# Per-pair reads for the output chains of a fused attention and ReGLU kernel, sixteen semaphores for the oT copies, and another static order

## The chip, the cores and the metric

The kernel runs on one core of a Trainium2 chip. The core has five engines that each work through an instruction queue of their own, in order: PE (TensorE, matrix multiplication; the profile shows its weight loads apart, as PEld), ACT (ScalarE), DVE (VectorE), POOL (GpSimd) and SP (SyncE, which here only issues DMA transfers). Engines wait for one another and for transfers through semaphores. The metric is the time of one execution on the device in microseconds (us). For the kernel before, the median of three runs is 687.94 us (687.48 to 688.73). Times inside the profile are counted from the start of its span.

## The reference

The input x is 2048 rows of 512 bfloat16 values. It is normalised row by row (layer norm without weights), and two blocks read the result; the output is the sum of both and of x:

```python
xn = _layernorm(x, axis=-1)
return x + _A_ref(xn, A_wqkv, A_wo) + _B_ref(xn, B_W_gate, B_W_up, B_W_down)
```

Block A is attention with 32 heads of 16 channels: `qkv = xn @ wqkv`, scores `q k^T` times 16^-0.5, softmax over all 2048 keys without a mask, times v, and `@ wo`. Block B is a gated ReLU layer with 1792 hidden channels: `relu(xn @ W_gate) * (xn @ W_up)`, and `@ W_down`. For each of the 32 heads 2048 x 2048 exponentials are needed.

## The kernel before, in words

**Tiling.** The 2048 rows are four chunks (c4) of 512 query rows. Within a chunk the 32 heads are eight groups of four heads, named by gg (0 to 3) and ee (0, 1); within a group the keys are 16 tiles of 128. For a chunk, a group and a key tile the scores of four heads are a tile of 128 x 2048. Most of them are made in two halves: a *unit* is one such half, a score pair on PE (`score`, L1289) into 128 x 1024 of PSUM, and one exponential on ACT (L1365) from there into a ring of 16 buffers in SBUF. There are 718 units, numbered in the order in which ACT does them; "sc190" is the score of unit 190. For 83 further tiles (`quad`, L1312) the exponential is made on DVE and POOL by integer arithmetic on the bits of a bfloat16: DVE copies the scores with a bias (L1320), then DVE (L1339) or POOL (L1335) adds two shifts. Both kinds are then weights for the products with v (`pv_stream`, L1244).

**Half operations.** PE's array is used as an upper and a lower half of 64 rows, which work side by side. A half operation is four matmuls (64 x 32 weights, 512 columns) on one half, with four weight loads ahead of it. Nearly all of PE's work is cut in this way: scores, products with v, the projections of q (`proj_q`, L837) and k (`proj_k`, L863), the gated layer (`glu`, L992) and the output rows (`out_rows`, L1034). PE has 5573 such operations and 12 blank ones that fill pauses.

**Output rows.** `out_rows` makes 128 rows of the output (index i in a chunk of four) as one chain that adds up in one PSUM bank: 14 pairs of a hidden tile hT and a piece of W_down, then up to four pairs of oT (the normalised attention output of a group, in x_sb) and a piece Wo_p of wo. Each pair is two half operations. W_down comes in 14 loads of 128 KB, six into Wd and four each into Wk and Wv, once these are no longer needed; a single tile object, t_wd, stands for all 14, and t_wo for the four loads of Wo_p. In the last chunk two of the row tiles (i = 1, 3) also add x through an identity pair, and end in `stream_out` (L1173), which the change leaves.

**Attention output.** When a group is done, `normalise` (L1188) copies the sums out of PSUM, sends the row sums through DRAM (streams n1, n2), and broadcasts the reciprocals back into rb with a transfer of 256 KB (stream n3, L1219). POOL multiplies (L1227, L1232). For the second group of each gg four small transfers of 16 KB (stream pk, L1234) bring the rows into oT. The q projections go through such copies of 16 KB too (L859, qT<-qf).

**What sets the order.** All operations are made as a graph of 8236 operations plus 12 blanks. The order of each queue and the places of the buffers come from a string, PLAN (L122 to L218), which `run` (L324) decodes; no planner runs at build time. `emit` (L380) then puts a wait wherever an operation depends on one whose semaphore its engine has not yet seen at that value, directly or through another engine. A half operation with weights waits for the writers of its weights ahead of its weight loads. `wait` (L476) emits one wait for each semaphore:

```python
for s, v in best.values():
    eng.wait_ge(s, v)
```

Each DMA stream has one semaphore; a load without a stream's name has one of its own, as each of the 14 loads of W_down and the four of Wo_p. Before a transfer of a stream is issued, the operations that read the transfer before it in that stream must have come far enough: SP waits for them. SP issues all transfers in one order.

**The opening.** x comes in as eight loads of one row tile (m = 0 to 7), two of two and one of four. wqkv comes as small parts for the first heads (Wq at L668, Wk at L669, 128 KB each), Wv (L672, 512 KB) and the rest of Wk and Wq (L685, L686, 384 KB each). PE transposes the normalised tiles of x (L764, through the identity), makes k and q for the first heads (L926) and then the first scores.

## Time and profile before

| what | value |
|---|---|
| median of three runs | 687.94 us |
| time of the profiled execution | 686.07 us |
| its span, first to last instruction | 684.2 us |
| PE busy | 675.6 us (99%) |
| PEld busy | 345.9 us (51%) |
| ACT busy | 666.8 us (97%) |
| DVE busy | 598.5 us (87%) |
| POOL busy | 499.8 us (73%) |
| granted TensorE clock, mean | 0.999 |

How to read the rows that follow in the prediction. A row of a timeline starts with the start in us from the start of the span and the length in us; then come engine, line of the kernel, operation, output<-inputs, number of instructions in the row, and in brackets the idle time of the engine before it with what ended it ("issue": nothing that the profile shows). Rows that begin with a line give a group: the shortest, median and longest duration in ns and the first and last start. A row with a window (from:to) gives the length, then busy time of PE, PEld, DVE, ACT and POOL with the number of instructions, the granted clock, the share of the DMA engines and GB/s. A row of a transfer ends with KB each and the median us from issue to landing. Matmuls overlap, so a row's length is that of a run of several.

### The profile page before, as it was taken

The numbers are of one execution on the slowest core, as the hardware profiler recorded it, in microseconds if no ns is written. First come the engines' busy times: TensorE is split into PE (matmuls) and PEld (weight loads), VectorE is DVE, ScalarE is ACT, GpSimd is POOL, SyncE is SP. The second block draws the span as 40 slices with busy tenths as digits, with TensorE's granted clock in tenths as the row PEclk, the third lists the DMA queues.
The fourth block names the chain that finished last, engine by engine and source line by source line (L and its number), as shares of the span: only waits on it lengthen the run. The fifth ranks groups of instructions, "written<-read, shape, count | busy, mean of one in ns | idle before, by whom it ended". The sixth has DMA issues, their size and how long they took to land.

```text
span 684.2 us, 45020 instructions
## 1 busy us (share of the span) xinstructions
PE 675.6 (99%) x22262; PEld 345.9 (51%) x19654; DVE 598.5 (87%) x1012; ACT 666.8 (97%) x730; POOL 499.8 (73%) x507
## 2 busy tenths in 40 slices
PE   8999999999999999999999999999999999999998
PEld 4455454545555554554444455554554455555543
DVE  9958899999989787999999788889998887988875
ACT  6999999999999999999999999999999999999994
POOL 3323768678688778887587886888878868787792
PEclk9999999999999999999999999999999999999999
DMA  7430220113122021212101022120202012131011
GB/s 216 57 75 12 58 77 27 33 55 91 56 65 66 5 77 34 69 41 63 35 23 31 10 78 63 38 69 5 56 27 61 25 53 62 44 86 42 22 36 54
DMA packets 55940, 35.86 MB, mean 52 GB/s; under 512 B 19336, under 2 KB 51784, under 8 KB 55752
## 3 DMA queue, kind: packets, MB, share of 16 engines
q1 hardware_dynamic: 55464, 32.71, 17.4%
q8 instruction: 164, 2.69, 1.6%
q10 hardware_dynamic: 288, 0.26, 0.1%
q14 instruction: 24, 0.20, 0.1%
HBM read 26.35 MB, written 2.35 MB: 42 GB/s over the span
## 4 chain that ended last, share of the span: by engine, by line
PE 75%; ACT 18%; DVE 5%; issue 1%; DMA 0%; POOL 0%; ACTq 0%
PE ps L250 75%; ACT ring L1365 18%; DVE stats L726 1%; DVE qd L1320 1%; DVE xn_sb L739 1%; DVE v_aug L876 0%; DMA x_sb<-in_A_x_dram 0%; DVE qT L952 0%; DVE mv L727 0%; ACT xn_sb L1164 0%; DVE qd L1339 0%; DVE xnT L780 0%; POOL rstd L721 0%; DVE xnT L1075 0%; DVE kT L869 0%
## 5 line engine op out<-in xcount | busy, mean ns | idle before, releaser
L1365 ACT ACTIVATE ring<-ps 128x1024 bf16<-128x1024 f32 x718 | 660.4, 1141 | 2.9 <-PE ps L250 2.5
L1335 POOL TENSOR_TENSOR qd<-qd,ints 128x512 int32<-128x512 int32 x446 | 450.5, 1041 | 143.8 <-DVE qd L1339 73.2
L250 PE MATMUL ps<-qT,kT 64*32 64x512 bf16 x8192 | 448.7, 374 | 1.3 <-DVE qd L1320 0.4
L1320 DVE TENSOR_SCALAR qd<-ps 128x512 int16<-128x512 f32 x612 | 396.7, 685 | 51.9 <-PE ps L250 49.0
L250 PE MATMUL ps<-qd,v_aug 64*32 64x512 bf16 x3672 | 263.0, 375 | 1.1 <-issue 0.9
L250 PE MATMUL ps<-ring,v_aug 64*32 64x512 bf16 x2872 | 236.5, 374 | 0.1
L1300 PEld LDWEIGHTS <-kT 64*32 64x32 bf16 x7584 | 151.1, 92 | 126.6 <-issue 32.6
L1272 PEld LDWEIGHTS <-v_aug 64*32 64x32 bf16 x4544 | 108.7, 91 | 75.6 <-issue 20.4
L250 PE MATMUL ps<-xnT,wgs 64*32 64x512 bf16 x1792 | 137.6, 374 | 0.0
L250 PE MATMUL ps<-xnT,wus 64*32 64x512 bf16 x1792 | 136.4, 374 | 0.0
L250 PE MATMUL ps<-Wd,hT 64*32 64x512 bf16 x768 | 59.0, 375 | 0.0
L810 PEld LDWEIGHTS <-wgs 64*32 64x32 bf16 x1792 | 43.1, 91 | 31.5 <-issue 7.4
L810 PEld LDWEIGHTS <-wus 64*32 64x32 bf16 x1792 | 43.2, 91 | 29.8 <-issue 7.6
L1339 DVE TENSOR_SCALAR qd<-qd 128x2048 int16<-128x2048 int16 x83 | 56.1, 690 | 2.3 <-PE ps L250 2.2
L810 PEld LDWEIGHTS <-hT 64*32 64x32 bf16 x1792 | 40.2, 92 | 28.2 <-issue 4.2
L250 PE MATMUL ps<-Wv,hT 64*32 64x512 bf16 x512 | 45.7, 375 | 0.0
L250 PE MATMUL ps<-Wk,hT 64*32 64x512 bf16 x512 | 42.8, 375 | 0.4 <-DVE qd L1320 0.3
L1020 DVE SCALAR_TENSOR_TENSOR hT<-ps,up_sb 128x512 bf16<-128x512 f32 x56 | 38.4, 685 | 4.6 <-PE ps L250 4.2
L1016 DVE COPY up_sb<-ps 128x512 f32<-128x512 f32 x56 | 38.4, 685 | 3.1 <-PE ps L250 2.5
L250 PE MATMUL ps<-Wo_p,x_sb 64*32 64x512 bf16 x480 | 40.2, 374 | 0.6 <-issue 0.5
L250 PE MATMUL ps<-xnT,Wq 64*32 64x512 bf16 x480 | 36.2, 375 | 0.0
L250 PE MATMUL ps<-xnT,Wk 64*32 64x512 bf16 x480 | 35.0, 374 | 0.3 <-DVE xnT L780 0.3
(70 smaller groups left out, 263.8 us busy)
## 6 DMA issues: line engine op xcount, KB each, us to landing
rb<-rec_scr SPq DMA_DIRECT2D x31, 256.0 KB
wus<-in_B_W_up_dram SPq DMA_DIRECT2D x38, 128.0 KB, 2.8
wgs<-in_B_W_gate_dram SPq DMA_DIRECT2D x38, 128.0 KB, 3.3
xr_sb<-in_A_x_dram SPq DMA_DIRECT2D x16, 128.0 KB, 2.6
qT<-qf SPq DMA_DIRECT2D x120, 16.0 KB, 2.6
out_dram<-xn_sb SPq DMA_DIRECT2D x14, 128.0 KB, 2.0
x_sb<-in_A_x_dram SPq DMA_DIRECT2D x8, 128.0 KB, 2.8
x_sb<-oT SPq DMA_DIRECT2D x60, 16.0 KB, 2.5
```

The lines of the kernel that those rows point to most:

```text
L250: return e.add_instruction(mybir.InstMatmult(name=e.bass.get_next_instruction_name(), engine=mybir.EngineType.PE, ins=[e.lower_ap(x), e.lo ...
L726: G.op("DVE", 580, lambda e, m=m: e.bn_stats(stats[:, m, :], xs(m)), reads=[t_xm[m]], writes=[t_st], prio=pr, order=last_xn if m == 4 else ())
L739: G.op("DVE", 320, lambda e, m=m, t=t_n: e.tensor_scalar(xn_sb[:, t.slot, :], xs(m), mv[:, m, 0:1], rstd[:, m:m + 1], op0=ALU.subtract, op ...
L810: e.ldweights(w()[rows, 32 * j:32 * j + 32], tile_position=(rows.start, 32 * j))
L1016: G.op("DVE", 603, lambda e: e.tensor_copy(up_sb[:, tup.slot, :], bank_of(tu)), reads=[tu], writes=[tup], prio=-590)
L1020: G.op("DVE", 603, lambda e: e.scalar_tensor_tensor(out=hT[:, th.slot, :], in0=bank_of(tg), scalar=0.0, in1=up_sb[:, tup.slot, :], op0=ALU ...
L1272: e.ldweights(vs(j), tile_position=(64 * half, 32 * j))
L1300: e.ldweights(ks(m), tile_position=(64 * half, 32 * m))
L1320: G.op("DVE", 601, lambda e, j=j, tx=tx: e.tensor_scalar(qd[:, tq.slot, 512 * j:512 * j + 512], ps[:, BANK[tx.slot], :], IBIAS[3], 0.0, op ...
L1335: G.op("POOL", POOL_NS / POOL_PIECES + 60, lambda e, x=x, n=n, c=slice(i * m, i * m + m): e.tensor_tensor(x().bitcast(I32)[:, c], raw().bi ...
L1339: G.op("DVE", 600, lambda e, n=n, x=x: e.tensor_scalar(x(), raw(), float(SHIFTS[n + 1]), None, op0=ALU.add), reads=[ti, tq], writes=[t], p ...
L1365: exp_ops[u] = G.op("ACT", 904, lambda e, tr=tr, k0=k0: e.activation(ring[:, tr.slot, :, :], ps[:, 4 * k0:4 * k0 + 2, :], ACTF.Exp, scale= ...
```

## The change: what it does

Three edits in the code, and another PLAN.

1. `mm_chain` takes a list of reads for each pair, where it is given one, and not only one list for the whole chain.
2. `out_rows` gives such lists: a pair with W_down reads its own hT tile and t_wd; a pair with Wo_p reads its own oT and t_wo; the identity pair reads its x rows and the identity. Before, each half operation of the chain read all of them.
3. The copies into oT use 16 streams (four for the partitions, four for gg) and not eight.

```diff
+            each = isinstance(reads[0], list)
...
+                mine = reads[i] if each else reads
                 for half in ((0, 1) if mode == "half" else (None,)):
                     fn, load = chain_part(w, x, lambda: bank_of(tile, sub), half, flags)
-                    G.op("PE", 216, fn, reads=reads, joins=[tile],
+                    G.op("PE", 216, fn, reads=mine, joins=[tile],
...
-                         load=load, weights=reads if weights is None else weights)
+                         load=load, weights=mine if weights is None else weights)
...
-            pairs, reads = [], [t_wo]
+            pairs, reads = [], []
             if first:
-                reads += [t_h[(c4, ft)] for ft in range(FT)] + [t_wd]
                 for ft in range(FT):
                     pairs.append(...)
+                    reads.append([t_h[(c4, ft)], t_wd])
             for g in gs:
                 to = t_oT[(c4, g)]
-                reads.append(to)
+                reads.append([to, t_wo])
...
+                reads.append([txr, t_id])
...
-                mm_chain(t, pairs, reads + [txr, t_id], pr, slots=slots, flags=flags)
+                mm_chain(t, pairs, reads, pr, slots=slots, flags=flags)
...
-                    stream=("pk", j, (n // 2) % 2), name="pk")
+                    stream=("pk", j, (n // 2) % 4), name="pk")
```

The new PLAN holds the same operations and as many blanks. Decoded and laid beside the old one:

- Of ACT's 731 operations all keep their place; of PE's 5573, 2286; of DVE's 1012, 791; of POOL's 503, 153; of SP's 429, 42. The shifts on average are 1.7 places on PE, 0.4 on DVE, 1.5 on POOL and 5.1 on SP; the largest are 106, 12, 28 and 47.
- 315 operations of PE stand in another unit. 143 of the 718 units hold another number of half operations. Units whose longer half holds five or more: 104 before, 98 after (20 of the 104 go, 14 others come).
- The first chain of chunk 0 starts in unit 226 (230 before), that of chunk 1 in unit 401 (402 before); the others start where they did. The first Wo_p pair of chunk 0 stands in unit 234 (237 before), that of chunk 1 in unit 404 (402 before).
- SP around unit 180: the broadcast of 256 KB that stood between two of the q copies for unit 190 stands behind them.
- The q copy with the least room stands in unit 489 for a score of unit 495 (471 before).
- The opening on SP, before: x0, x1, x2, x3, Wq, Wk, x4, x5, x6, x7, Wv, x8-9, x10-11, x12-15, rest of Wk, rest of Wq. After: x0, x1, x2, x5, x3, x4, x6, Wk, x7, Wq, x8-9, x10-11, x12-15, rest of Wq, rest of Wk, Wv.
- The opening on PE, before: the last four transposes stand in a row between the scores of units 2 and 3. After: the scores of units 1 to 5 stand between and behind them (only the last two transposes stay together). Seven blanks stand ahead of the first transpose, three before. The first half operation that reads Wv has place 51, 47 before.

More of the change, by code (lines that the diff above doesn't have):

```diff
@@ new lines @@
+    "cRBe3`v7izZ7n25-1k{zSRg-OUHhNre!~NXo5O5hiYegVn$H~HIP)hOqg%u1${eBl))61N9L9A>f5H0NyfB~EL0^g`b#rNBUhBeUna?i&g>5s&GjauEF>X4`jDuw{be|!9lZ<bn%jtCPA0<9@%Q)j("
+    "->$hFXFjQLYYyW9E;gncUvu-mdDAcsHs8Yx6gS;yOlVw42iX=jrxDYc7rJ@VKcQE(1x<`HT?YAtF^}IOX^>?(x1u8caAWJzFS=qTmtx-bU76l6Y&Lyh%xT2lG*;X)O_i5MJm9y3{_?2erfy`7&wG~d"
+    "ZQ0L#Nvr!EXPD>Po8fD28fgYfE+v<@PtI)tFiY5<qTJkwF^%+qFR@aYFW_P`TxYiM$VH9ZV9F;&X%q+<Y^1e6mHGdcoiDC(cFVcks#kf}3$xr5FJ$H^mI=(9#LN8;`fA-Q53@F`>@(uejJb>udLagR"
+    "<xaec!W1vFO>gd-zG7a58N2YBi+Rm_7kB7!?i<L(G~$B!QphX?Gbnz*vROtqQXBy=!wplJ*W5EVlZW{s%xmSD_(`lMzm!XxgN*Q5!0u%}m(X7+&SZy38u^rN6pC~M^P3=Y$S{MP#LR`{1%1ewePQOl"
@@ new lines @@
+    "yn~fEzQVRAxNl++0kJ*9$wmSsJHUnYUOApwA>igFt*v<(*{dWwlbt$X7I6Tu_{qh*_8Ot(!gzBInOf2#+}s;CZkx_!()qfs8V^W|%=GY@uxl=20Ff+B7{1lDWHs3-7(!$cStTFzS^y*FHgZ7PB!(!)"
+    "*0{_<qbv+Rn|2#%FEi1|KrZ8HIL7Z6ZVa-92Jnr)^a7ZMTVrGuG8<y}S;j0Z=An;dmjc5V<~pXGrpKhU<X0;OhUKyvxYydRfs84d;WwKv$Vc3_Q*KK|BR1SjPcLl7`%=gtIVH)ZBylIqx;2YhhMSxC"
+    "ZK)HZwu}(LH<3XPMi#;c8ZsB<y1EfB%VW9`b7qpP0<oOrT$3M6)RNC~U9r$gV6L&AC?v1QWv2Mc$QL;tpwVo}ZewlZLONNHjiLlVzfBGC0EHB&g8YyipsW0%klO?nhY!pGfHyF4xL=i+Ldrk0Vil~^"
+    "c7`(*y8!(}+R0HcW9)m@FB~m7<d=IkLgw6}an7v@*G*Wq%SL0gIo9uA8<qIYH$tUzpX%a%WolLp?4C1z)cu5Sr+2O>wr$uJF$PJD_Iu5e#CD2RY*X0S&o<65K?nDXTkhYQZ#(8KQ=#!d^Av8^^E^<?"
```

182 lines of the change are left out of this document (87 added, 95 removed).

## The prediction

> **What bounds the kernel now.** I read the page first (engines, chain, groups), then ACT's timeline around each stop, and there the timelines of PE's weight loads and of SP. The page:
>
> ```profile
> span 684.2 us, 45020 instructions
> PE 675.6 (99%) x22262; PEld 345.9 (51%) x19654; DVE 598.5 (87%) x1012; ACT 666.8 (97%) x730; POOL 499.8 (73%) x507
> PE 75%; ACT 18%; DVE 5%; issue 1%; DMA 0%; POOL 0%; ACTq 0%
> L1365 ACT ACTIVATE ring<-ps 128x1024 bf16<-128x1024 f32 x718 | 660.4, 1141 | 2.9 <-PE ps L250 2.5
> ```
>
> PE is named in three quarters of the chain and ACT is busy 97% of the span: both are nearly full, so the chain's shares don't say what a change is worth. The 718 exponentials of L1365 do. Their spacing, from ACT's timeline in a stretch without stops, and their first and last start:
>
> ```profile
> L1365 ACT ACTIVATE ring<-ps x718: 1017/1146/1314, 10.9 to 673.1; 128x1024 bf16<-128x1024 f32 x180
> 516.07 14.85 ACT L1365 ACTIVATE ring<-ps 128x1024 bf16<-128x1024 f32 x16
> 528.73 3.11 ACT L1365 ACTIVATE ring<-ps 128x1024 bf16<-128x1024 f32 x3
> ```
>
> The last two rows come from two windows: the second begins with the first one's fifteenth exponential, so (528.73-516.07)/14 = 0.904 us apart. 717 intervals at 0.904 make 648.2; the stream takes 673.1-10.9 = 662.2. So ACT loses 14.0 us to stops; 10.9 us lie before it and 684.2-673.1 = 11.1 behind its last start. A change pays here only if it removes stops of the exponentials or shortens those two ends. Times below are lost ACT time: the distance of two starts less 0.904 for each.
>
> **The change part by part.**
>
> *A. The waits at the start of an output chain.* Before, every half operation of out_rows reads one list (all 14 hT tiles, all of Wd, all of Wo_p, all oT copies). Thus the first half op of a chunk's chain waits for every semaphore of the list that PE has not yet seen. The rows of ACT and of the weight loads at the four chunk starts:
>
> ```profile
> 222.85 2.08 ACT L1365 ACTIVATE ring<-ps 128x1024 bf16<-128x1024 f32 x2
> 225.36 1.02 ACT L1365 ACTIVATE ring<-ps 128x1024 bf16<-128x1024 f32 x1 [0.42 <-PE ps L250]
> 381.54 1.21 ACT L1365 ACTIVATE ring<-ps 128x1024 bf16<-128x1024 f32 x1
> 383.77 1.94 ACT L1365 ACTIVATE ring<-ps 128x1024 bf16<-128x1024 f32 x2
> 540.73 3.02 ACT L1365 ACTIVATE ring<-ps 128x1024 bf16<-128x1024 f32 x3
> 542.54 2.13 ACT L1365 ACTIVATE ring<-ps 128x1024 bf16<-128x1024 f32 x2
> 631.49 3.01 ACT L1365 ACTIVATE ring<-ps 128x1024 bf16<-128x1024 f32 x3
> 632.51 1.07 ACT L1365 ACTIVATE ring<-ps 128x1024 bf16<-128x1024 f32 x1
> 224.21 0.12 PEld L810 LDWEIGHTS <-hT 64*32 64x32 bf16 x4 [0.73 <-DVE qd L1320]
> 382.40 0.12 PEld L810 LDWEIGHTS <-hT 64*32 64x32 bf16 x4 [0.68 <-DVE qd L1320]
> 541.80 0.12 PEld L810 LDWEIGHTS <-hT 64*32 64x32 bf16 x4 [0.43 <-DVE qd L1320]
> 631.36 0.34 PEld L810 LDWEIGHTS <-hT 64*32 64x32 bf16 x9 [0.36 <-DVE qd L1320]
> ```
>
> Chunk 0: 225.36-222.85 is two intervals and 0.70 more. Chunk 1: 383.77-381.54 is 0.42 too long for two. Chunk 2: 542.54-540.73 loses nothing. Chunk 3: 632.51-631.49 loses 0.12. The sum is 1.24. The DVE step that the rows name (qd, a score copy) has nothing to do with hT; the weight load was last in a row of waits. By the code chunk 0 has 16 DMA semaphores there: eight for Wd (six of its own, and one each for the part in Wk and the part in Wv, whose loads wait for one another), four for Wo_p, four for the oT copies. Chunks 1 to 3 have the eight semaphores of the copies and one or two of engines. The idle time goes with that number: 0.73 for sixteen, 0.36 to 0.68 for eight and a few.
>
> After the change a Wd half op waits for its own hT and for Wd. t_wd is still one tile of 14 loads, so chunk 0's first half op, now at unit 226 instead of 230, keeps eight DMA semaphores. Its first Wo_p half op, at unit 234, gets the four of Wo_p and four copies: eight again. The next three pairs have four copies each, since the copies now use 16 streams and not eight. (On SP that costs nothing: a copy there waits for a reader of the copy before it in its stream, which is now the one of the same heads a chunk earlier, read long before.) In chunks 1 to 3 the chain starts on hT alone, and each Wo_p pair waits for four copies. Queued behind such a wait on PE are the score half ops of the next units, and so ACT. Two groups of eight at the price of chunk 3 cost 2 x 0.12; groups of four I take at 0.05 in all (their nearest row, chunk 2, lost nothing). A = -1.24 + 0.24 + 0.05 = -0.95. Bounds: -1.24 if all of it hides as in chunk 2; 0 if the two groups and the groups of chunk 1 each cost the 0.42 of chunk 1 (1.26 against 1.24).
>
> *B. The q copies before unit 190.* SP's order, the landing times of such copies, and what ACT and PE did:
>
> ```profile
> 178.53 0.58 SPq L1219 DMA_DIRECT2D rb<-rec_scr  x1
> 179.15 1.16 SPq L859 DMA_DIRECT2D qT<-qf  x2
> DMA to landing us min/median/max: 1.7/2.6/5.6
> 184.97 0.41 PE L250 MATMUL ps<-qT,kT 64*32 64x512 bf16 x4 [0.40 <-DVE qd L1320]
> 184.65 1.09 ACT L1365 ACTIVATE ring<-ps 128x1024 bf16<-128x1024 f32 x1
> 186.10 1.02 ACT L1365 ACTIVATE ring<-ps 128x1024 bf16<-128x1024 f32 x1 [0.37 <-PE ps L250]
> ```
>
> The landing row is that of tile qT. The second copy was issued at about 179.7, behind a broadcast of 256 KB (rb), and the score that reads it ran at 184.97, some 5.2 us later, at the slow end of 1.7 to 5.6. ACT lost 186.10-184.65-0.904 = 0.55. The new order puts the broadcast behind these copies. It has its own reader on POOL (the multiplications of normalise), which has no exponential behind it directly. I take -0.45: 0.1 remains. Bounds: -0.55, and +0.55 if another copy gets the same stop, since nearly all of SP's instructions (387 of 429) change places.
>
> *C. The small stops.* Two rows of PE's timeline with score half ops give the length of a step:
>
> ```profile
> 12.01 0.38 PE L250 MATMUL ps<-qT,kT 64*32 64x512 bf16 x8
> 13.64 0.60 PE L250 MATMUL ps<-qT,kT 64*32 64x512 bf16 x16
> ```
>
> Eight matmuls are one step of both halves of the array, sixteen are two, and these take 0.22 longer. PE's two halves run side by side, so a unit (the work between two scores) takes as many steps as its longer half has. In 104 units of the old order that is five or more: at least 5 x 0.22 = 1.10 against ACT's 0.904. The new order has 98 (20 go, 14 come). Six fewer at 0.2 would give -1.2 if nothing covered them; but a shorter unit beside a long one covers some, so I take a third, -0.4. Bounds: -1.2, and +1.2 if those that come are uncovered and those that go were covered. POOL (350 of 503 instructions in other places) and DVE (221 of 1012) I cost at 0 within this term: POOL has slack (73% busy), and where that cover is gone the scores' copies on DVE are late next, at the same 0.2 a stop.
>
> *D. The opening.*
>
> ```profile
> 3.62 1.93 SPq L655 DMA_DIRECT2D x_sb<-in_A_x_dram  x4
> 8.49 1.03 SPq L686 DMA_DIRECT2D Wq<-in_A_wqkv_dram  x1
> Wq<-in_A_wqkv_dram SPq DMA_DIRECT2D x1, 384.0 KB, 7.6
> x_sb<-in_A_x_dram SPq DMA_DIRECT2D x2, 128.0 KB, 3.4
> 8.59 1.06 PE L926 MATMUL ps<-xnT,Wq 128*32 128x384 bf16 x32
> 10.91 2.87 ACT L1365 ACTIVATE ring<-ps 128x1024 bf16<-128x1024 f32 x3
> 12.33 1.36 PE L764 MATMUL ps<-ident,xn_sb 128*128 128x128 bf16 x16
> 14.10 3.82 ACT L1365 ACTIVATE ring<-ps 128x1024 bf16<-128x1024 f32 x4 [0.32 <-PE ps L250]
> 15.12 0.38 PE L250 MATMUL ps<-Wv,xnT 64*32 64x512 bf16 x4
> 15.00:16.20 1.20, 1.11 (x48) 0.67 (x48) 1.20 (x4) 1.20 (x3) 0.00 (x0) 1.00 0.09 29
> ```
>
> Gain: four transposes in one piece (12.33) hold the score of unit 3; 14.10-10.91 is three intervals and 0.48. The new order puts scores between them (only the last two stay together); I count -0.3, since DVE's and PE's work there is only spread. Loss: the small load of Wq moves from fifth to tenth in SP's queue. The x loads of the same size at that place (issued by 3.62+1.93) land after 3.4, so Wq at about 5.1+3.4 = 8.5 to 9.0, where the projection began at 8.59: 0 to 0.4, I take 0.2. Wv moves from the eleventh place to the last load. The last place now (Wq's rest, issued 8.49) lands 7.6 later at 16.1; the first Wv half op ran at 15.12 and has four places more before it, so about 15.5. PE then stands up to 0.6 us; the scores of units 4 and 5, which the new order puts ahead of that half op, give ACT two more exponentials (1.8 us), which covers half of it: +0.3. Behind 16.2 the queue is empty (the last row: DMA share 0.09). D = -0.3+0.2+0.3 = +0.2; bounds -0.5 (both loads in time) and +0.9 (no gain, 0.4 and 0.5 lost).
>
> [...]
>
> *E. Stops without a cause in the order.*
>
> ```profile
> 406.70 1.03 ACT L1365 ACTIVATE ring<-ps 128x1024 bf16<-128x1024 f32 x1
> 408.64 1.02 ACT L1365 ACTIVATE ring<-ps 128x1024 bf16<-128x1024 f32 x1 [0.92 <-PE ps L250]
> 407.51 0.09 PEld L1272 LDWEIGHTS <-v_aug 64*32 64x32 bf16 x1 [1.18 <-issue]
> ```
>
> The largest single stop (408.64-406.70-0.904 = 1.04) has "issue" as its cause: PE waited for nothing that the profile shows. The diff adds no instruction to PE except where waits move, so I cost this at 0, with ±1.0 because such a stop can fall elsewhere. The tail (stream_out, which the diff leaves) I cost at 0 too; its cover is that its half ops still read Wo_p and Wo_l as one list.
>
> Sum: A -0.95, B -0.45, C -0.4, D +0.2 = **-1.6 us**. The profiled run took 686.07, of which 684.2 is the span; it lies 1.87 below the median of 687.94, so I move the median: 687.94-1.6 = **686.3 us**. The bounds, added as they stand, are -4.5 and +3.7.
>
> **The rivals.**
>
> *Late copies (slower).* SP is one queue in order, and the new order shortens margins: the copy with the least (a q copy of unit 495) is issued 6 units ahead of its score (24 before), 6 x 0.904 = 5.4 us, against landings of up to 5.6 us in tile qT's row. If copies or weights come late like that of 184.97, each costs 0.55. Three such stops use up the 1.6; from six on the kernel is slower by the 0.2% (1.4 us) that a measurement here can tell from no change. Six give 687.94-1.6+3.3 = 689.6. For it: SP's order is new nearly throughout. Against it: only one stop of that kind stands in the trace of before, and the median landing is 2.6.
>
> *The waits only move (no difference).* The change then doesn't do what it says: chunk 0 keeps eight semaphores twice, and B's stop goes to another copy; then A is 0, B 0, C -0.4, D +0.2: 687.7. For it: the row of chunk 1, 0.42 with as few semaphores. Against it: chunks 2 and 3, with about as many, lose 0 and 0.12.
>
> *The order removes many small stops (faster by more).* Of the 14.0 us, the stops named above (1.24, 0.55, 0.48, 1.04) are 3.3; 10.7 remain in small pieces. If a quarter of these goes (2.7) in place of the 0.4 of C, the time is 687.94-1.6-2.3 = 684.0. For it: 143 of the 718 units get another number of half ops, so there is room for it. Against it: only 315 of 5573 PE instructions change their unit, and the number of units with five steps falls by six alone.
>
> **How the numbers follow.** Chances: the sum as it stands 0.44 (its own range 685.3 to 687.5), late copies 0.20, waits only move 0.16, many small stops 0.20. Faster by over 0.2%: all of the last and three fifths of the first, 0.47; slower: 0.20; the rest, 0.33, is within 0.2%. The range goes from 683.4 (a third of the small-stops case lies below) to 689.4 (somewhat over half of the late-copies case lies above), leaving out a little under 2 in 10.
>
> **What would show it.** A: no idle time of 0.6 before a weight load of hT in units 226 to 232 and 401 to 404; instead idle of 0.4 or less at the first hT load of chunk 0 and at its first x_sb load. B: no gap in the exponentials near 185. C: ACT's first-to-last start about 1.5 shorter than 662.2. D: an unbroken row of exponentials from the first to the sixth, or else a gap before the first Wv half op near 15.5. It is wrong if scores wait for q copies at new places, if ACT's first start moves beyond 11.4, or if stops of "issue" come to more than the one of 407.5 and its like.

## The result, and the profile after

The changed kernel takes 691.95 us in the median of six runs (690.60 to 693.70), against 687.50 for six runs of the kernel before beside it: a ratio of 1.0062 with a 95% interval of 1.0047 to 1.0077. It is slower by about 4.3 us, where 1.6 us less was forecast. The profiled execution took 691.17 us, 689.4 of it span, 5.2 more than before.

The page of the changed kernel (span, busy times, chain by engine, the group of the exponentials; L1368 is what L1365 was), and the row of the exponentials' line with shortest, median and longest duration and the first and last start:

```profile
span 689.4 us, 45023 instructions
PE 678.6 (98%) x22262; PEld 350.6 (51%) x19650; DVE 599.9 (87%) x1012; ACT 668.4 (97%) x730; POOL 499.8 (73%) x507
PE 91%; DVE 2%; POOL 2%; issue 1%; DMA 1%; ACT 1%; SPq 0%; ACTq 0%; POOLq 0%
L1368 ACT ACTIVATE ring<-ps 128x1024 bf16<-128x1024 f32 x718 | 662.2, 1138 | 4.9 <-PE ps L250 3.8
```

```profile
L1368 ACT ACTIVATE ring<-ps x718: 1018/1146/1316, 12.3 to 678.2; 128x1024 bf16<-128x1024 f32 x180
```

The busy times hardly move, and POOL, which had 0% of the chain, now has 2%. The first exponential starts 1.4 later and the last 5.1 later. To see where, I took the start of each exponential from the trace, subtracted 0.904 per interval, and added what is left over stretches of units. This table serves all the runs below; its columns are the first start, the four stretches, what lies behind the last start, and the span (one profiled execution each, us):

| kernel | first start | units 1-40 | 41-198 | 199-219 | 220-717 | tail | span |
|---|---|---|---|---|---|---|---|
| before | 10.91 | 1.14 | 3.36 | 0.32 | 9.18 | 11.11 | 684.2 |
| after | 12.27 | 1.96 | 2.27 | 1.60 | 11.93 | 11.17 | 689.4 |
| e1 changed code, old order | 11.84 | 1.11 | 3.00 | 0.32 | 10.98 | 11.04 | 686.5 |
| e2 new order, old opening | 11.79 | 1.07 | 2.97 | 2.05 | 12.02 | 11.17 | 689.2 |
| e3 new order, three blanks | 11.23 | 2.96 | 2.58 | 3.87 | 10.32 | 11.18 | 690.3 |
| e4 new order, 128 more | 13.33 | 1.91 | 3.38 | 2.10 | 8.32 | 11.21 | 688.4 |
| e5 new order, one copy earlier | 11.75 | 1.95 | 2.44 | 0.23 | 9.17 | 11.61 | 685.3 |
| e6 old opening, copy earlier | 11.51 | 1.19 | 2.85 | 0.11 | 10.58 | 11.17 | 685.6 |
| e7 as e6, 128 more | 11.09 | 1.13 | 3.91 | 0.18 | 7.67 | 12.07 | 684.2 |
| e8 before, 128 more | 11.13 | 0.98 | 2.97 | 0.40 | 11.43 | 11.03 | 686.1 |
| e9 old order, copy late | 11.51 | 1.13 | 2.58 | 3.57 | 10.96 | 11.04 | 689.0 |
| e10 as e6, 64 more | 11.68 | 2.03 | 2.76 | 0.38 | 9.25 | 11.17 | 685.4 |
| e11 as e6, 192 more | 11.68 | 1.10 | 3.27 | 0.23 | 8.73 | 11.18 | 684.3 |
| e12 as e6, more transfers | 11.03 | 1.38 | 5.63 | 0.10 | 14.89 | 11.16 | 692.4 |

After against before: the opening with the first 40 units +2.2, units 41 to 198 -1.1, units 199 to 219 +1.3, the rest +2.75. The gains lie at the places of A and B. The losses come from three causes: the opening, one oT copy with what follows from it, and the "issue" stops.

**The places of A and B** look as they should. ACT's rows at the q copies of unit 190 and at the two chain starts, then the first weight loads of hT and x_sb there (chunk 0, chunk 1):

```profile
179.00 13.98 ACT L1368 ACTIVATE ring<-ps 128x1024 bf16<-128x1024 f32 x15
221.49 11.25 ACT L1368 ACTIVATE ring<-ps 128x1024 bf16<-128x1024 f32 x12
378.74 13.99 ACT L1368 ACTIVATE ring<-ps 128x1024 bf16<-128x1024 f32 x15
222.59 0.12 PEld L810 LDWEIGHTS <-hT 64*32 64x32 bf16 x4 [0.31 <-issue]
229.39 0.12 PEld L810 LDWEIGHTS <-x_sb 64*32 64x32 bf16 x4
383.66 0.10 PEld L810 LDWEIGHTS <-hT 64*32 64x32 bf16 x4
386.73 0.12 PEld L810 LDWEIGHTS <-x_sb 64*32 64x32 bf16 x4 [0.25 <-issue]
```

The exponentials run on in all three stretches. The first hT load of chunk 0 stands 0.31 with its eight semaphores where it stood 0.73 with sixteen; chunk 1's hT starts without a wait, and its x_sb load stands 0.25. In PE's trace these waits are instructions of their own (EVENT_SEMAPHORE), two semaphores each and 0.106 us apart: six ahead of the load at 224.21 before, two ahead of the one at 222.59 after. The even steps show that none of them had to wait for anything; their number is the cost.

**The opening.** ACT, then PE (L910 and L1383 are the warm-up and the blanks), then SP's issue of Wv and its landing in the changed kernel; the last fence is the first transpose of the kernel before:

```profile
12.27 5.61 ACT L1368 ACTIVATE ring<-ps 128x1024 bf16<-128x1024 f32 x6
18.30 2.08 ACT L1368 ACTIVATE ring<-ps 128x1024 bf16<-128x1024 f32 x2 [0.42 <-PE ps L250]
5.43 2.54 PE L1383 MATMUL ps<-Wo_l 128*128 128x512 bf16 x7
7.81 0.61 PE L764 MATMUL ps<-ident,xn_sb 128*128 128x128 bf16 x8
17.00 0.38 PE L250 MATMUL ps<-Wv,xnT 64*32 64x512 bf16 x4
8.22 1.30 SPq L672 DMA_DIRECT2D Wv<-in_A_wqkv_dram  x1
Wv<-in_A_wqkv_dram SPq DMA_DIRECT2D x1, 512.0 KB, 7.6
```

```profile
5.52 0.40 PE L764 MATMUL ps<-ident,xn_sb 128*128 128x128 bf16 x4
```

The seven blanks hold PE until 7.81, so the first transpose comes 2.3 later than before; its input had been written at 5.65. Wv lands at 8.22 + 7.6 = 15.8, and ACT has a first stop of 0.61 at its seventh exponential. PE does not wait for Wv there: ahead of 17.00 stand two blanks and a pause for ACT.

**One oT copy.** Units 199 to 219 lost 1.28 more. SP, POOL and ACT of the changed kernel there, with PE's row between; L1239 is the copy into oT, L1222 the broadcast n3, L1219 the transfer n2, L1235 POOL's multiplication:

```profile
185.72 0.47 SPq L1219 DMA_DIRECT2D rec_scr<-rrec  x1
190.27 0.57 SPq L1222 DMA_DIRECT2D rb<-rec_scr  x1
190.88 0.57 SPq L1239 DMA_DIRECT2D x_sb<-oT  x1
195.81 1.28 POOL L1235 TENSOR_TENSOR oT<-o_sb,rb 128x512 bf16<-128x512 f32 x1 [2.44 <-DMA x_sb<-oT]
208.81 0.38 PE L250 MATMUL ps<-qd,v_aug 64*32 64x512 bf16 x4 [0.44 <-POOL qd L1338]
209.44 1.02 ACT L1368 ACTIVATE ring<-ps 128x1024 bf16<-128x1024 f32 x1 [0.24 <-PE ps L250]
```

And of the kernel before, the same copy (first of the two) and the same multiplication:

```profile
163.58 2.15 SPq L1236 DMA_DIRECT2D x_sb<-oT  x2
191.11 1.29 POOL L1232 TENSOR_TENSOR oT<-o_sb,rb 128x512 bf16<-128x512 f32 x1 [0.66 <-DVE qd L1339]
```

The copy, one of the four of chunk 0's first group, is issued at 190.88 where it was issued at 163.58: it stands behind n2 and n3, and n3 makes SP stand until n2 has landed (4.1 us here). The multiplication of unit 190's group writes the buffer that this copy reads, so POOL stands 2.44 for it. Behind it in POOL's order are the shifts of quad 200; PE waits for one of them with a product at 208.81, and the exponentials of units 212 and 213 come 0.35 and 0.30 late.

The larger part of the 1.60 came another way: unit 201 lost 0.76. DVE, PE and ACT of the changed kernel, and in the second fence the same shift on DVE before:

```profile
195.85 1.80 DVE L1342 TENSOR_SCALAR qd<-qd 128x2048 int16<-128x2048 int16 x1
198.30 0.59 PE L250 MATMUL ps<-qT,kT 64*32 64x512 bf16 x12 [0.57 <-DVE qd L1323]
198.98 10.23 ACT L1368 ACTIVATE ring<-ps 128x1024 bf16<-128x1024 f32 x11 [0.50 <-PE ps L250]
```

```profile
194.94 0.68 DVE L1339 TENSOR_SCALAR qd<-qd 128x2048 int16<-128x2048 int16 x1
```

By the code (`port` in `run`) POOL's shifts and multiplications wait for DVE's last shift, but a shift on DVE does not wait for POOL. Here DVE's shift starts 0.04 us behind the late multiplication, takes 1.80 us where the median of the 83 is 0.68, and ends 0.55 after the multiplication has. The score copy behind it is late, and so is a score. A second shift, at 207.94, takes 1.36 beside a shift on POOL. Such a shift of over 1.3 us stands in the traces of all five kernels with the late copy (after, e2, e3, e4, e9) and in none of the nine others, whose longest is under 1.0. So part of the copy's price is that POOL, once late, meets DVE.

**The "issue" stops.** The largest single loss of the changed kernel is 0.96 at unit 441. ACT's row, PE's row, and the page's row of the queue that fetches instructions (number of packets, MB, share):

```profile
422.13 3.77 ACT L1368 ACTIVATE ring<-ps 128x1024 bf16<-128x1024 f32 x4 [0.82 <-PE ps L250]
421.25 0.37 PE L250 MATMUL ps<-qd,v_aug 64*32 64x512 bf16 x1 [0.67 <-issue]
q8 instruction: 164, 2.69, 1.7%
```

PE broke off inside a row of four matmuls (three are there at 420.19) and waited for nothing the profile shows. PE and PEld have 22262 + 19650 = 41912 instructions on the page, and 41912/164 is about 256; 2.69 MB in 164 packets are 16 KB each. In the traces of before and after every packet of this queue has 16384 bytes, and from the start of one to the start of the next PE starts 256.0 and 255.6 instructions on average, its waits counted. So I read it as one fetch of 16 KB for each block of 256 of PE's instructions. Numbered in PE's order, nearly all such stops lie at numbers of about 190 to 202 within a block of 256, in every run. At them PE goes on 1.2 to 1.6 us after the end of a fetch, and at none of these borders in the two traces sooner (the least is 1.27 before, 1.20 after), as if a block could be used only then. By this reading stops at such borders cost the exponentials 2.2 us before and 6.5 after: 0.49 at unit 238, 0.45 at 242, 0.76 at 315, 0.96 at 441, 0.55 at 586, 0.52 at 603, and smaller ones. Two of these are not borders alone. At 238 and 586 PE stands at the waits for the copies of a Wo_p pair, and a border falls on them:

```profile
232.40 0.12 PEld L810 LDWEIGHTS <-x_sb 64*32 64x32 bf16 x4 [0.69 <-issue]
```

In the same order with the border elsewhere (e4) the two units lose 0.02 and 0.12. The sums below also depend on the counting: they take the stops from 0.05 us in the 2.7 us behind such a pause; taken from 0.14 us in 1.8 us they are 2.1 before and between 1.8 and 6.5 in the other traces without added traffic.

### The profile page after: what moved, and what is told of

It is laid out like the page before. It is cut to its first block, busy times and chain, and to the rows that moved or that the text cites. A ratio compares the mean times of both kernels' runs of the same rounds, so it can differ in the third digit from the quotient of the medians.

```text
span 689.4 us, 45023 instructions
## 1 busy us (share of the span) xinstructions
PE 678.6 (98%) x22262; PEld 350.6 (51%) x19650; DVE 599.9 (87%) x1012; ACT 668.4 (97%) x730; POOL 499.8 (73%) x507
## 3 DMA queue, kind: packets, MB, share of 16 engines
q8 instruction: 164, 2.69, 1.7%
## 4 chain that ended last, share of the span: by engine, by line
PE 91%; DVE 2%; POOL 2%; issue 1%; DMA 1%; ACT 1%; SPq 0%; ACTq 0%; POOLq 0%
PE ps L250 90%; POOL qd L1338 2%; DVE qd L1323 1%; DMA wgs<-in_B_W_gate_dram 1%; PE ps L910 1%; ACT ring L1368 1%; DMA rec_scr<-rrec 1%; PE ps L1383 0%; DVE v_aug L878 0%; DVE stats L726 0%; DVE xn_sb L739 0%; ACT qT L953 0%; PE ps L928 0%; POOL oT L1235 0%; POOL x_sb L1230 0%
## 5 line engine op out<-in xcount | busy, mean ns | idle before, releaser
L1368 ACT ACTIVATE ring<-ps 128x1024 bf16<-128x1024 f32 x718 | 662.2, 1138 | 4.9 <-PE ps L250 3.8
L250 PE MATMUL ps<-Wd,hT 64*32 64x512 bf16 x768 | 61.3, 375 | 0.0
L1342 DVE TENSOR_SCALAR qd<-qd 128x2048 int16<-128x2048 int16 x83 | 58.1, 711 | 2.3 <-PE ps L250 2.1
L250 PE MATMUL ps<-Wk,hT 64*32 64x512 bf16 x512 | 45.5, 375 | 0.0
## 6 DMA issues: line engine op xcount, KB each, us to landing
rb<-rec_scr SPq DMA_DIRECT2D x31, 256.0 KB
```

The lines of the kernel that those rows point to most:

```text
L250: return e.add_instruction(mybir.InstMatmult(name=e.bass.get_next_instruction_name(), engine=mybir.EngineType.PE, ins=[e.lower_ap(x), e.lo ...
L1342: G.op("DVE", 600, lambda e, n=n, x=x: e.tensor_scalar(x(), raw(), float(SHIFTS[n + 1]), None, op0=ALU.add), reads=[ti, tq], writes=[t], p ...
L1368: exp_ops[u] = G.op("ACT", 904, lambda e, tr=tr, k0=k0: e.activation(ring[:, tr.slot, :, :], ps[:, 4 * k0:4 * k0 + 2, :], ACTF.Exp, scale= ...
```

## Experiments

Ratios are to the kernel before, with a 95% interval, from three to five rounds beside it; each group below ran on one chip, e5 to e8 on another than e1 to e4, and e9 to e11 on a third. So kernels of different groups are better compared by their ratios than by their medians. The kernel before's median was 688.15 beside e1 to e4, 687.89 beside e5 to e8, 687.85 beside e9 to e11 and 687.04 beside e12.

**e1: the code without the order.** PLAN is the old one, in the changed code.

```diff
 mm_chain, out_rows, normalise: as changed
-PLAN (new)
+PLAN (old)
```

> The changed code (reads per pair, sixteen streams) with the order of before. If the waits are worth what step A says and the loss lies in the new order, the stops of 0.70 and 0.42 us at the chain starts of chunks 0 and 1 go, and the time is 0.5 to 1.2 us under that of before (686.3 to 687.0). If the waits per pair are what costs (rival), it is 2 us or more over before. If they only move, it is within 0.3 us of before.

Measured: 688.38 (687.48 to 690.23), ratio 1.0002 [0.9991, 1.0013]. The waits only moved: chunk 0 lost 0.70 in unit 231 and chunk 1 0.42 in unit 403 before, and here ACT loses 0.29 in unit 231 and then, where the copies are first waited for, 0.73 in unit 238:

```profile
230.92 0.35 PEld L809 LDWEIGHTS <-x_sb 64*32 64x32 bf16 x8 [0.52 <-issue]
232.55 3.77 ACT L1367 ACTIVATE ring<-ps 128x1024 bf16<-128x1024 f32 x4 [0.55 <-PE ps L249]
```

Chunk 1 keeps 0.09 of its 0.42, and unit 586, at the copies of chunk 2, loses 0.41 (0.14 before). The loss of the after-kernel is in its order. It also shows that the first exponential of one and the same opening lies between 10.91 (before) and 11.84 (e1), so part of the 12.27 is chance: in the warm-up the matmuls start 0.427 us apart and from some point 0.216, and that point came at 4.2 us in the trace of before, at 7.0 in e1, at 7.2 in after. So between before and e1, two traces of one opening, it moved by nearly 3 us; what sets it is not shown. With nearly the same point, e1 and after differ by 0.43 in the first start and by 1.28 with units 1 to 40.

**e2: the new order with the old opening**, spliced at PE's 104th operation (about unit 11).

```diff
 PLAN: the first 104 operations of PE, 57 of DVE, 21 of ACT, 16 of SP, 13 of POOL
-in the new order (seven blanks, Wv last)
+in the old order (three blanks, Wv eleventh)
```

> The changed kernel, but up to about unit 11 all queues have the order of before; behind it the new order. Theory: the opening costs 1.4 us ahead of the first exponential (12.3 against 10.9) and 0.6 to 0.8 behind it, so the time is 1.8 to 2.4 us under the changed kernel (about 689.5), and still 1 to 3 over before, from stops at the borders of instruction blocks. Rival (late copies, small stops by the new order alone): the opening is worth under 0.5 us and the time stays at 691.5 or more.

Measured: 689.22 (687.09 to 692.24), ratio 1.0016 [1.0000, 1.0033]. The new opening costs 2.7 us in the medians and 3.2 by the ratios. In the table, first start and units 1 to 40 together are 14.23 after and 12.86 here. Units 199 to 219 still lose 2.05.

**e3: the new order without four of the seven blanks** ahead of the first transpose.

```diff
-PLAN_OPS = 8248
+PLAN_OPS = 8244
```

> The changed kernel with four of the seven blanks ahead of the first transpose left out. Theory: the first transpose starts when its input is there (about 5.7 instead of 7.8), and the first exponential 0.9 to 1.6 us earlier (10.7 to 11.4), the whole run as much faster. Rival (the opening is bound by the loads of Wk and Wq, and by DVE): the first exponential stays at 12.0 or later and the time does not move.

Measured: 691.31 (689.24 to 694.65), ratio 1.0045 [1.0028, 1.0062]. The blanks alone aren't the opening's loss. ACT, and PE's first Wv half op:

```profile
11.23 5.61 ACT L1367 ACTIVATE ring<-ps 128x1024 bf16<-128x1024 f32 x6
18.54 2.10 ACT L1367 ACTIVATE ring<-ps 128x1024 bf16<-128x1024 f32 x2 [1.70 <-PE ps L249]
17.26 0.38 PE L249 MATMUL ps<-Wv,xnT 64*32 64x512 bf16 x4 [0.74 <-DMA Wv<-in_A_wqkv_dram]
```

The first exponential is 1.04 earlier (part of it by chance, since PE's pace changed at 6.4 us here and at 7.2 in after) and the seventh is 0.24 later: PE now waits for Wv, the last load. What the blanks hold back, the load would hold back.

The 3.87 that this run loses in units 199 to 219 are not all the copy's. Rows of the windows around PE's stop there (the column after POOL's is the granted clock):

```profile
207.70:209.70 2.00, 0.21 (x4) 0.00 (x0) 1.76 (x2) 1.14 (x2) 2.00 (x2) 1.00 0.30 77
209.90:211.10 1.20, 1.20 (x42) 0.79 (x36) 0.36 (x1) 0.66 (x1) 1.20 (x2) 1.00 0.51 123
211.20:214.50 3.30, 3.30 (x72) 2.22 (x65) 2.19 (x4) 2.31 (x3) 1.94 (x3) 0.50 0.15 41
```

About 1.3 us after PE went on, its clock was at half for 3.4 us, and units 213 to 215 lost 1.78 in it.

**e4: the changed kernel, with 128 small PE instructions more in the warm-up**, so that every border of 256 falls elsewhere in the order.

```diff
-            for _ in range(10):
+            for _ in range(8):
                 ins = e.matmul(ps[:, BANK[0], :], Wo_l[:, 0, 0:128], zeros, start=True, stop=True)
+            for j in range(4):
+                e.ldweights(Wo_l[0:64, 0, 32 * j:32 * j + 32], tile_position=(0, 32 * j))
+            for k in range(128):
+                j = k % 4
+                ins = matmul_loaded(e, ps[32 * j:32 * j + 32, BANK[0], 0:8], Wo_l[0:64, 0, 32 * j:32 * j + 32],
+                                    zeros[0:64, 0:8], True, True, (0, 32 * j))
```

> The changed kernel with 128 more small PE instructions ahead of the first blank (two of the ten warming matmuls left out for them), so that every border of a block of 256 instructions falls half a block later in the work; the order is the same. Theory (PE stops where a block's fetch ends under about a us before PE gets there): the stops at 237, 305, 421, 555, 571 and 591 us go, and others may come at new places, again at places that are 256 instructions apart; the sum of such stops, 5.1 us before, may be anything from 2 to 6. Rival (these stops belong to the work there: a wait, a buffer, the clock): they stay at the same units (242, 315, 441, 586, 603, 624).

Measured: 689.92 (688.83 to 690.34), ratio 1.0020 [1.0008, 1.0033], 2.0 us less than the changed kernel in the medians and 2.9 by the ratios. The stops at units 242, 315, 441, 586 and 603 are gone; others came at 172 (0.41), 265 (0.76), 482 and 483, 588 and 695. Border stops sum to 3.5 in place of 6.5. The stop at unit 212 stays (1.77): it has another cause.

**e5: one transfer moved.** The copy of above goes ahead of n2 in SP's queue; nothing else changes.

```diff
 SP's order (new PLAN), around unit 190's group
+x_sb<-oT   (pk, j = 1, first group of chunk 0)
 rec_scr<-rrec   (n2)
 rb<-rec_scr     (n3)
-x_sb<-oT   (pk, j = 1, first group of chunk 0)
```

> The changed kernel with one transfer moved: the oT copy that POOL's multiplication near 196 us waited for (pk, j = 1, of the first gg of chunk 0) is issued ahead of the n2 transfer behind which SP stood, some 5 us earlier. Theory: POOL multiplies 3 us earlier, its shifts are in time, and the stop at units 212 to 215 (1.8 us in the runs with the old opening and with three blanks, 0.65 in the changed kernel's profile) goes; the median falls by 0.6 to 2 us, to about 690. Rival (POOL is late there whatever the copies do, because of the new order of its own queue): unit 212 stops as before, and the time does not move.

Measured: 688.61 (687.12 to 692.14), ratio 1.0020 [1.0005, 1.0034], 3.3 us less than the changed kernel in the medians and 2.9 by the ratios. SP, POOL and ACT:

```profile
186.02 0.52 SPq L1238 DMA_DIRECT2D x_sb<-oT  x1
192.97 1.28 POOL L1234 TENSOR_TENSOR oT<-o_sb,rb 128x512 bf16<-128x512 f32 x1
196.96 19.50 ACT L1367 ACTIVATE ring<-ps 128x1024 bf16<-128x1024 f32 x21
```

POOL no longer waits, and units 199 to 219 lose 0.23.

**e6: old opening and moved copy together** (the edits of e2 and e5).

```diff
 PLAN: as e2
+copy moved as in e5
```

> The new order with the old opening and with that copy moved. Theory: against the old opening alone (689.2) the 1.8 us of unit 212 go, so about 687.5, level with before or a little under it. What is left against before is then the stops at block borders (6.4 us in the run with the old opening, 2.2 in that of before). Rival: the rest of the order loses too, and it stays over 689.

Measured: 686.72 (685.22 to 690.02), ratio 0.9990 [0.9979, 1.0001]. Against e2 the copy is worth 2.5 us in the medians and 1.8 by the ratios, against e5 the opening 1.9 and 2.1. With both faults out, the new order is level with the kernel before or a little ahead.

**e7: e6 with the 128 small instructions of e4.**

```diff
 PLAN: as e6
+warm-up as in e4
```

> The same kernel with 128 more small PE instructions ahead of everything, so that block borders fall half a block later. Theory of block borders: stops at 586, 603 and 658 (0.68, 0.42, 0.69 with the old opening alone) go, others come; the sum of border stops differs by 1 to 3 us from the kernel without the shift, and the median with it, less about 1 us for the later warm clock. Rival (the borders don't matter): the same stops at the same units, the same median to 0.3 us.

Measured: 686.29 (684.46 to 687.88), ratio 0.9973 [0.9961, 0.9984]: faster than both kernels. Its exponentials:

```profile
L1372 ACT ACTIVATE ring<-ps x718: 1018/1151/1315, 11.1 to 672.1; 128x1024 bf16<-128x1024 f32 x180
```

Border stops sum to 3.2 against 4.0 in e6, 0.8 less in the profiled executions; the medians differ by 0.43, and the intervals of the two ratios overlap. The 1 us expected for the later warm clock, an estimate (the first exponential of e4 starts 1.06 behind that of after), did not show: here it starts at 11.09, in e6 at 11.51.

**e8: the kernel before with the same 128 instructions.**

```diff
 before
+warm-up as in e4
```

> The kernel before with the same 128 small PE instructions and no other change. Theory of block borders: its stops at units 165, 267, 429 and 450 (2.1 us) go, and new ones come at other places, in all 2 to 6 us; the median moves by 0.5 us or more, more likely up, since the order of before was made with its own borders where they were. Rival: the stops stay at these units, and the median moves by the 0.3 to 1 us that the opening loses.

Measured: 687.83 (686.40 to 690.07), ratio 0.9999 [0.9983, 1.0014]. The three large "issue" stops of before (units 165, 267, 429, the last the 1.04 of the prediction) are gone, and 145 (0.41), 435 (0.82), 622 (0.52) and 626 (0.39) came; the sum rose from 2.2 to 3.2. So here a border stop belongs to the place that a border falls on, not to the work there, and a shift is no gain in itself.

**e9: the reverse of e5.** Old order in the changed code (e1), with only that copy moved back behind n3.

```diff
 SP's order (old PLAN), around unit 190's group
-x_sb<-oT   (pk, j = 1, first group of chunk 0)
 rec_scr<-rrec   (n2)
 rb<-rec_scr     (n3)
+x_sb<-oT   (pk, j = 1, first group of chunk 0)
```

> The changed code with the old order, as in the first experiment (688.38 us), but with one transfer of SP moved: the oT copy that stood far ahead of the sums' transfers n2 and n3 of unit 190's group stands directly behind them, as in the new order. Theory (that place of one copy is the main loss): POOL's multiplication waits 2 to 3 us for it, the shift of quad 200 behind it comes late, ACT stops once or several times between units 200 and 216, and the median rises by 2 to 3 us over 688.38, to 690.4 to 691.4 (ratio 1.003 to 1.005). Rival (the late copy costs only together with other places of the new order): POOL stands idle too, but ACT does not stop there, and the median is 688.0 to 689.0.

Measured: 691.92 (688.71 to 694.09), ratio 1.0052 [1.0036, 1.0068]: 3.5 us above e1 (3.4 by the ratios), a little more than expected. SP, POOL, PE, ACT:

```profile
191.46 0.56 SPq L1238 DMA_DIRECT2D x_sb<-oT  x1
196.28 1.28 POOL L1234 TENSOR_TENSOR oT<-o_sb,rb 128x512 bf16<-128x512 f32 x1 [6.05 <-DVE qd L1341]
209.26 0.38 PE L249 MATMUL ps<-qd,v_aug 64*32 64x512 bf16 x4 [2.18 <-POOL qd L1337]
210.11 1.02 ACT L1367 ACTIVATE ring<-ps 128x1024 bf16<-128x1024 f32 x1 [1.91 <-PE ps L249]
```

POOL stands 6.05 (the row names DVE, whose result had been there as in e5; the copy had just been issued at 191.46), and the chain POOL, PE, ACT follows: 0.52 in unit 203 and 2.04 in unit 212. With e5 this settles it: the place of one transfer of 16 KB costs 1.8 to 3.4 us by the ratios (2.5 to 3.5 in the medians), in either order. In the table, column 199-219 is 1.6 to 3.9 in the five kernels with the late copy and 0.10 to 0.40 in the nine others. The granted clock, which is on record for every execution, goes with the copy as well: it was 0.998 or less in 29 of 51 executions of the five kernels, and in 5 of 190 of the others (before among them). In e9 the seven executions with it had a median of 692.44 and the four without 690.86. One stretch of 3.4 us at half clock, as in the trace of e3, makes 0.9975 of a mean; that it lay behind PE's stop in the executions without a trace is not shown.

**e10 and e11: e6 with 64 and with 192 small instructions.**

```diff
-            for k in range(128):
+            for k in range(64):    # e10; 192 in e11
```

> The new order with the old opening and the copy moved ahead, as in the sixth and seventh experiments, but with 64 small PE instructions more in the warm-up in place of 0 and 128. Theory (stops without a cause sit at every 256th PE instruction, and what a border costs depends on what stands there): all such stops lie at PE instruction numbers of 194 to 202 in a block of 256, counted with the shift, thus at other units than in the two runs before; their sum lies between 2.5 and 6.5 us, and the median between 685.5 and 688.0. Rival (the stops belong to the units, and the shift only by chance took some away): they fall in the same units as with shift 0, and the median is 686.7 within 0.4.

> As the run before, with 192 small PE instructions. Theory: stops at the shifted borders, in units that the runs with shift 0, 64 and 128 do not show, their sum between 2.5 and 6.5 us, and a median between 685.5 and 688.0, apart from the others by what the sum of the border stops differs. Rival: the same units as with shift 0, median 686.7 within 0.4.

Measured: e10 687.35 (684.90 to 689.38), ratio 0.9984 [0.9970, 0.9998]; e11 686.54 (685.39 to 689.66), ratio 0.9978 [0.9961, 0.9995]. The stops of this kind keep to the same numbers within a block. (Three larger "issue" stops of all the runs do not, and their cause was not found: 1.41 us at unit 229 of e8, 0.66 at 579 of e10 and 1.92 at 426 of e12.) In e6 the larger ones fall on units 43, 441, 471, 586, 603 and 611, in e10 on 6, 42, 432, 601, 618, 622 and 626, in e11 on 52, 167, 272, 451 and 625. The sums are 4.0, 4.0 and 3.1. So four placements of the borders over one order (e6, e10, e7, e11) give 0.9990, 0.9984, 0.9973 and 0.9978, the mean 0.9981. That they move was as the theory has it. That the medians differ by the sums isn't shown: the differences lie within the intervals.

**e12: what makes a block late.** e6 with every load of the gate and up weights issued twice, the second time into DRAM that nothing reads.

```diff
+                        def more(e, src=src, dt=dt):
+                            e.dma_start(junk[...], src[...]).then_inc(G.more_sem, 16)
-                        paced(lambda e, ...: e.dma_start(
+                        paced(lambda e, ...: more(e) or e.dma_start(
```

> The kernel of the sixth experiment (new order, old opening, copy moved ahead), in which every load of the gate and up weights is issued a second time by SP, from the same source into a piece of DRAM that nothing reads; PE's instructions are the same and at the same places. It asks what makes a block of PE's instructions arrive late. Theory (other transfers on the same DMA engines delay the start of a fetch): of the 163 borders more than the 33 of the sixth experiment have their fetch end less than 1.55 us before PE goes on, 45 to 70; the exponentials lose 5 to 9 us at borders in place of 4.0, and the median rises by 1.5 to 5 us over 686.72. Rival (fetches come late for another reason, such as PE running through a block quickly): 25 to 40 such borders, 3 to 5 us lost there; the median rises by less than 1 us, unless copies on SP come late too, which would show as stops away from the borders.

Measured: 693.60 (691.43 to 694.25), ratio 1.0088 [1.0060, 1.0115], by the ratios 6.7 us above e6. The traffic of e12 and, in the second fence, of e6 (packets, MB, share of 16 engines):

```profile
q1 hardware_dynamic: 76136, 42.68, 22.3%
340.15 2.02 ACT L1374 ACTIVATE ring<-ps 128x1024 bf16<-128x1024 f32 x2 [1.11 <-PE ps L249]
83.92 0.09 PEld L813 LDWEIGHTS <-wus 64*32 64x32 bf16 x4 [1.10 <-DMA wus<-in_B_W_up_dram]
```

```profile
q1 hardware_dynamic: 55464, 32.71, 17.3%
```

With 10 MB more, ACT loses 8.1 us at borders in place of 4.0 (1.26 at unit 351, the second row), with the same PE instructions at the same places. Of the 163 borders 44 have their fetch end less than 1.55 before PE goes on; 33 in e6. That is just under the 45 expected, the loss within the 5 to 9, and the median above what was expected, because other transfers came late too: the weights of a gated unit at 83.92 (0.90 lost) and a stop of 1.92 at unit 426 away from any border. The count alone shows nothing, since after has 46 without the traffic; the loss of 8.1 does lie above the 2.2 to 6.5 of every trace without it. The traces without added traffic point the same way: over 2135 borders of thirteen of them the median fetch began 0.84 us after the border before it where the other transfers used under 5% of the DMA engines in the next 1.5 us, and 1.24 where over 50%. So in these traces a fetch begins later beside other transfers; that this alone made the 8.1 is not shown. Why the fetches of the changed kernel came later than those of before (46 of 163 within 1.55 us, 23 before; 33 to 40 in e1, e5, e6 and e9) isn't settled by this: each figure is from one execution.

## Why the prediction was wrong, step by step

**The step that failed first: what waits on SP's transfers.** A said of the new streams that on SP they cost nothing, B said of POOL's multiplication that it "has no exponential behind it directly", and C costed POOL's order at 0, "POOL has slack (73% busy)". Each looks at one queue and stops there. POOL's multiplication writes the buffer that an oT copy reads, so it waits for that copy; the copy waits on SP behind n3, and n3 for n2; behind the multiplication on POOL stand shifts, behind a shift stands a product on PE, and behind that the scores; beside the late POOL a shift on DVE takes 1.80 us where the median is 0.68, and behind that stand scores too. The term missing was +1.8 to +3.4 us, larger than any in the sum, and the mean slack of POOL didn't cover it: e9 has POOL stand 6.05 for a single copy. The late copies rival had the queue right and the victim wrong. It priced a q copy that a score reads, 0.55 each, and needed six of them; it was one oT copy, read at leisure on PE but holding a buffer. The prediction listed SP's order around unit 180 and q copies by their margin to a score; no margin was worked out from a copy to the next writer of its source.

**D, the opening, +0.2 with bounds -0.5 to +0.9: measured 1.9 to 2.7 in the medians, 2.1 to 3.2 by the ratios.** The four more blanks ahead of the first transpose had no term at all, though the change listed them; at the slower pace of the warm-up, 0.427 each, they are 1.7 us of PE. Wv was seen as late (to land at 16.1 and be asked for at 15.5; it landed at 15.8 and was first used at 17.00), but covered by two exponentials; e3 shows that blanks and load are not two terms to be added, since with the blanks gone the wait for Wv takes the same time. The observation to make it wrong, a first start beyond 11.4, came (12.27), but it was a poor sign: the unchanged opening has 11.84 in e1, and the 10.91 of before goes with the earliest change of PE's pace in the fourteen traces.

**E, stops without a cause, 0 ± 1.0: measured 6.5 us against 2.2 in the profiled executions.** "The diff adds no instruction to PE" was true and not enough. By the reading above the stops are borders of instruction blocks, they moved in the runs with small instructions put ahead of them (e4, e8, e10, e11), and their sum was 2.2 to 6.5 over thirteen traces with unchanged traffic. By this count the 2.2 of before is the lowest of the thirteen, and the eleven experiments without added traffic have 3.9 on average; by the narrower count four traces lie at about 2. That, and the early change of PE's pace (4.2 us), may be why its profiled execution lay 1.87 below the median; no trace of another of its executions was kept. Seen from the median the term of another order is then near 0, as forecast, but its bound is some ± 2.5 and not ± 1.0.

**A and B, -0.95 and -0.45: right at their places, within a smaller total.** The stops of 0.70, 0.42 and 0.55 are gone in the changed kernel and in e6, and eight semaphores cost 0.31 of PE's time and none of ACT's. The +0.05 for the groups of four copies was too small where a border meets them: units 238 and 586 lose 0.49 and 0.55 after (e4: 0.02 and 0.12). But e1 shows that the waits as such only move, as the second rival had it (688.38 against 688.15); the order around them, not the shorter lists alone, took the stops away. B's reading of the kernel before holds: the last part of that q copy landed at 184.91, and the score started at 184.97. Unit 189 loses 0.76 in e4 and 0.41 in e7, but no q copy is waited for there, so that is another stop.

**C, -0.4: not seen.** Losses of 0.05 to 0.2 came 62 times after and 52 before, and those below 0.14 sum to 7.25 and 6.74 us. The fourth case, many small stops gone, did not come.

With the two faults repaired and four placements of the borders, A, B, C together come to a mean ratio of 0.9981, -1.3 us, against the -1.8 forecast for them. The sum failed by what it didn't hold.

## What to carry to other kernels

When an order changes, work out for every moved transfer two margins, not one: to the first reader of what it writes, and to the next writer of what it reads; then follow the waiting engine's queue on to the bound engine. An engine's mean slack says nothing of the one instruction that stands in front of the wrong other one, and an engine that comes late can meet another that it was ordered to avoid. And judge an order by several placements of its instruction blocks (here 64 to 192 idle instructions at the start): one placement carries some microseconds of chance (border stops of 2.2 to 6.5 us over thirteen traces here).

## What the runs showed of the hardware that was not expected

PE's instructions arrive, by the counts above, in blocks of 256, 16 KB each (164 fetches, 2.69 MB, for 41912), and where PE waited for one, it went on 1.2 to 1.6 us after the end of a fetch. A block takes PE about 4.0 us here, and its fetch began 0.8 to 1.0 us after the border before and took 1.0 to 1.1 (medians of the traces), so by these figures 0.3 to 1.0 us of margin is left. Beside other transfers the fetch began later (1.24 where they used over 50% of the DMA engines, 0.84 under 5%). Border stops cost 2.2 to 6.5 us per execution, up to about 1.0 at one, and 8.1 with 10 MB more traffic. At most of the 163 borders the exponentials lose nothing: a pause of PE with a loss of 0.05 or more behind it stands at 4 to 9 of them before and at 15 to 23 after, counted from pauses of 0.3 or of 0.1.

Two more things came with the late copy. A shift on DVE (0.68 us in the median) that began while POOL worked took 1.3 to 1.8 us in five traces. And in e3 PE's granted clock fell to 0.50 for 3.4 us, 1.3 us after a stop in which PE had stood idle for 1.90; e2, e4 and e9 have stops as long there (1.86 to 2.18) in their profiled executions, and the clock stayed at 1.00.
